# One written order from the first load to the end of stage two: a plan for stage one, sums of the scale in 64 columns, and differences of halves on GpSimd

## The chip, the cores and the metric

The kernel runs on one core of one Trainium2 chip. The metric is the time of one execution on the device in microseconds (us). A core has five engines that each work through a queue of their own in order: TensorE (PE in the profile, with its weight loads as PEld), VectorE (DVE), ScalarE (ACT), GpSimd (POOL) and SyncE (SP). SP, ACT and POOL also issue DMA transfers between DRAM and the on-chip memory (SBUF). Matrix products land in PSUM, 8 banks of 128 x 512 floats. An instruction waits by semaphore for what it reads, and for the buffer that it writes to come free; while it waits, everything behind it on its engine waits too.

## What is computed

```python
mod = (silu(c) @ w_mod).reshape(1, 6, 1, 512)          # c: (1, 512), w_mod: (512, 3072)
sa, ca, ga, sb, cb, gb = (mod[:, i] for i in range(6))
h = layernorm(x) * (1 + ca) + sa                       # x: (1, 2048, 512)
x = x + ga * irfft2(rfft2(h) * (w_r + 1j * w_i))       # a 2-D spectral filter
h = layernorm(x) * (1 + cb) + sb
x = x + gb * (mish(h @ w1 + b1) @ w2)                  # w1: (512, 1376), w2: (1376, 512)
```

## The kernel before

The 2048 rows are 128 partitions by 16 tiles n. The transforms are matrix products with constant matrices, in fp32 or as a high and a low fp32r part ("split"). There are three stages.

**Stage one** (the opening) goes over the 16 tiles. At the start the gate of `c` is made (`sc`), PE multiplies it with four pieces of `w_mod` (`scale_sums`, L333, 128 equal columns for each of four j into four banks), and DVE turns the constant `kr` into the scaled row transform `krs`, kr times one plus the sum (`scale_rows`, L338). `row_sums` multiplies ones by it, for the mean (`kb`). For each tile: loads of `x`, of the transposed `x` (`load_xt`) and of the column matrix `mraw` (`load_m`); PE's row transform (`p1_row`, L277, bank A or B); mean and variance on DVE and ACT (`norm_sums`, `first_guess`, `first_scale`); `p1_mean` on DVE; a high part (`p1_cast`, ACT) and a low part (`p1_low`, DVE, for the odd tiles in `POOL_LOW` on POOL inside `p1_cast`); the split of `mraw` into `mring` (`p1_split`: one cast on ACT, a difference and a negation on POOL); three groups of three matmuls in bank C (`p1_col`, L322 to L324); and a copy to `a_sb` (`p1_save`, L328, ACT). During the last tiles DVE sums the shift `sa` (`shift_sum`, L184), then PE transforms it (`shift_rows`, L348) and DVE keeps the part that each partition owns in `saz` (L355 and L357, first 16 columns, then 48).

**Stage two** (the middle) goes over 17 groups of columns of `a_sb`; group 0 is special, a full group has four columns and 512 elements. Group g passes through `turn_z` (four transposes on PE, L540), `copy_z` (ACT, L553), `p2_shift` (POOL adds `saz`, L558), `p2_mul` (PE with `kf`, L566), `lane` twice (ACT, L595 and L601), `other` (POOL times weights, L604), `own` (DVE times weights, L608), `p2_add` (DVE, L612), `fold` (step 0: difference of two halves, L622, on POOL for odd g below 15 and else on DVE; step 1 on DVE, L624), `spin_mul` and `spin_copy`, `p2_out` (PE, L480), and `store_d` twice (copies into `dd`, L458 on ACT, or L456 on DVE for the second copy of the groups in `FREE`). Between them the other vectors of `w_mod` are loaded (`mod_fetch`, SP) and summed (`mod_late`, L184, DVE), the filter's weights are reloaded (`load_wq`), and the gate `ga` goes through DRAM (`gate_flat`, `gate_spread`, L111) and is multiplied into `kiv` (`mod_gate`, L685, POOL).

**Stage three** transforms back (`p3_col`, L974; `p3_row`, L983, which reads `kiv`), normalizes again, and does the two dense layers with Strassen-like products (`up`, L1105; `down`, L1214) for the rest of the time.

What sets the order: inside `with tc.manual_schedule()` the instructions of an engine keep the order in which the program issues them. There are three such parts. Stage one's order is written out as a loop. The middle and the last stage are lists of steps (`Plan`), issued in the places that the long strings in `ORDERS` give. Between the three parts the framework's scheduler decides, so instructions of the next part can stand ahead of the end of the one before it.

Of the kernel before, what the change touches and what calls it, by code (L numbers as in the profile page):

```python
# [7 lines left out]
F32 = mybir.dt.float32  # L8
# [83 lines left out]
def tile_spectral_block(ctx: ExitStack, tc: tile.TileContext, x_d, w1_d, b1_d, w2_d,  # L92
# [156 lines left out]

    def load_all(n):  # L250
        load_xt(n)
        load_x(n)
        load_m(n)

    def load_rest():
        nc.sync.dma_start(kf, kf_d)
        nc.sync.dma_start(wz, wz_d)
        for i in range(4):
            nc.sync.dma_start(wqa[:, i], wq_d[i])
            if i == 1:  # L260
                nc.sync.dma_start(kv, kv_d)
# [33 lines left out]
    def p1_cast(n):  # L295
# [3 lines left out]
        if n in POOL_LOW:  # L299
            g = buf("t")  # L300
            if n == 1:
                nc.scalar.activation(gh, c, AF.Copy, scale=one)
# [1339 lines left out]
```

## Time and profile before

| | |
|---|---|
| median of three runs | 372.18 us (370.38 to 372.61) |
| profiled execution | 373.39 us, its span 371.6 |
| granted TensorE clock, mean | 0.994 |
| busy: PE, DVE, ACT, POOL | 355.2, 296.7, 248.3, 98.5 us |
| moved by DMA | 91.78 MB, mean 247 GB/s |
| loads of `x` and `xring` in stage one | 16 each, 256 KB, 4.8 us to landing |

A row of the profile names the line of the kernel (L322), the engine, the operation, what it writes and reads (buffer numbers left out) with shapes, and how often; then busy time and the mean in ns. A time in brackets is how long the engine had been idle before the instruction, and what ended that. "SPq" and "ACTq" are DMA issues on those queues. The granted clock is a share of full speed. Ends of matmuls are modelled, so a busy PE is not PE at its peak.

### The profile page before, as it was taken

How to read it: one execution, taken by the hardware profiler on the slowest of the kernel's cores; microseconds unless marked ns; L12 is line 12 of the kernel's file. 1: busy time of each engine (PE TensorE's matmuls, PEld its weight loads, DVE VectorE, ACT ScalarE, POOL GpSimd, SP SyncE). 2: the span in 40 equal slices, each digit the busy share in tenths (PEclk: the TensorE clock that was granted, in tenths of full speed). 3: DMA queues.
4: the chain of work that ended last, by engine and by line, in shares of the span. 5: the costliest groups of instructions: out<-in, count | busy, mean ns of one | idle time of the engine just before them, and what ended most of it. 6: DMA issues, size and time to landing. Idle time of an engine off the chain costs nothing.

```text
span 371.6 us, 7670 instructions
## 1 busy us (share of the span) xinstructions
PE 355.2 (96%) x2598; PEld 319.3 (86%) x2598; DVE 296.7 (80%) x708; ACT 248.3 (67%) x549; POOL 98.5 (27%) x156
## 2 busy tenths in 40 slices
PE   8999978898899999999999899999999999999995
PEld 8999955566699988788888789999999999999995
DVE  1898957998969889775777679998579895895896
ACT  1798848897378979884567696674676744545741
POOL 0578707776217360114202200004100000000000
PEclk9999989999999999999999999999999999999999
DMA  7999994565365997999999979767895986974023
GB/s 245 362 324 375 342 388 164 183 194 181 134 196 175 261 353 259 344 326 307 278 320 311 365 261 321 192 222 218 262 315 146 270 268 189 293 251 114 2 56 115
DMA packets 55639, 91.78 MB, mean 247 GB/s; under 512 B 7696, under 2 KB 21104, under 8 KB 55472
## 3 DMA queue, kind: packets, MB, share of 16 engines
q1 hardware_dynamic: 51168, 77.52, 62.6%
q0 software_dynamic: 2416, 7.87, 8.6%
q10 hardware_dynamic: 2016, 5.90, 5.2%
q8 instruction: 21, 0.34, 0.4%
q14 instruction: 18, 0.15, 0.1%
HBM read 70.03 MB, written 17.57 MB: 236 GB/s over the span
## 4 chain that ended last, share of the span: by engine, by line
PE 58%; DMA 14%; DVE 12%; ACT 4%; issue 4%; POOL 3%; SPq 3%; ACTq 0%; DVEq 0%; POOLq 0%
PE bank L1105 17%; PE bank L1214 17%; PE bank L1088 6%; PE bank L1206 4%; DMA modr<-in_B_w_dram 3%; DMA wm<-in_w_mod_dram 3%; PE bank L1151 3%; PE bank L1210 2%; DMA wqa<-in_w_q_dram 2%; PE bank L974 2%; PE bank L277 1%; PE bank L983 1%; DMA xring<-in_x_t_dram 1%; DMA x<-modr 1%; PE bank L333 1%
## 5 line engine op out<-in xcount | busy, mean ns | idle before, releaser
L1105 PE MATMUL bank<-hT,wr 128*128 128x256 f32 x360 | 51.5, 284 | 1.1 <-DMA wr<-w_S 1.1
L1105 PEld LDWEIGHTS bank<-hT,wr 128*128 128x128 f32 x360 | 47.0, 191 | 2.7 <-issue 0.9
L1105 PE MATMUL bank<-hB,wr 128*128 128x256 f32 x318 | 46.5, 285 | 1.9 <-ACT odd L1118 1.1
L1105 PEld LDWEIGHTS bank<-hB,wr 128*128 128x128 f32 x318 | 42.0, 191 | 4.3 <-ACT odd L1118 1.3
L1032 ACT CAST ah<-buf 128x512 fp32r<-128x512 f32 (+1 forms) x35 | 21.0, 607 | 13.5 <-PE bank L1214 6.7
L1273 POOL DMA_DIRECT2D x<-modr x5 | 4.4, 877 | 93.8 <-DVE buf L1175 27.8
L1033 DVE TENSOR_TENSOR al<-buf,ah 128x512 fp32r<-128x512 f32 (+1 forms) x35 | 23.4, 672 | 6.4 <-ACT ah L1032 6.3
L1214 PE MATMUL bank<-w2a,ah 128*128 128x256 f32 x119 | 25.9, 283 | 0.0
L1088 PE MATMUL bank<-hB,wr 128*128 128x512 f32 x96 | 24.2, 393 | 0.1
L1214 PE MATMUL bank<-w2b,ah 128*128 128x256 f32 x105 | 23.1, 283 | 0.0
L900 POOL DMA_DIRECT2D turned<-x x16 | 8.8, 564 | 48.0 <-DVE buf L1175 21.2
L1088 PEld LDWEIGHTS bank<-hB,wr 128*128 128x128 f32 x96 | 17.8, 188 | 4.1 <-ACT buf L976 0.6
L322 PE MATMUL bank<-buf,mring 128*128 128x512 f32 x48 | 20.7, 432 | 0.2 <-DVE buf L315 0.2
L1214 PEld LDWEIGHTS bank<-w2a,ah 128*128 128x128 f32 x119 | 19.8, 191 | 0.1
L1214 PEld LDWEIGHTS bank<-w2b,ah 128*128 128x128 f32 x105 | 17.9, 191 | 0.6
L480 PEld LDWEIGHTS bank<-kv,a_sb 128*64 128x64 f32 x252 | 13.6, 137 | 5.3 <-ACT d L458 2.4
L983 PE MATMUL bank<-kiv,buf 128*128 128x128 f32 x128 | 17.0, 278 | 0.6 <-DVE x L986 0.5
L974 PE MATMUL bank<-kc,d 128*128 128x128 f32 x128 | 16.7, 276 | 0.5 <-ACT d L458 0.5
L277 PE MATMUL bank<-modr,xring 128*128 128x128 f32 x128 | 16.7, 275 | 0.0
L1033 DVE TENSOR_TENSOR al<-even,ah 128x384 fp32r<-128x384 f32 (+1 forms) x15 | 8.7, 580 | 9.9 <-ACT ah L1032 9.9
L480 PE MATMUL bank<-kv,a_sb 128*64 128x128 f32 x252 | 15.7, 276 | 1.0 <-ACT a_sb L637 1.0
L1214 PE MATMUL bank<-w,ah 128*128 128x256 f32 x84 | 16.4, 284 | 0.0
(328 smaller groups left out, 1097.1 us busy)
## 6 DMA issues: line engine op xcount, KB each, us to landing
wr<-w_S SPq DMA_DIRECT2D x60, 256.0 KB, 4.1
wr<-w_A SPq DMA_DIRECT2D x45, 256.0 KB, 4.1
w_S<-hT SPq DMA_DIRECT2D x20, 256.0 KB, 4.1
x<-in_A_x_dram SPq DMA_DIRECT2D x16, 256.0 KB, 4.8
xring<-in_x_t_dram SPq DMA_DIRECT2D x16, 256.0 KB, 4.8
w_A<-wr SPq DMA_DIRECT2D x15, 256.0 KB, 4.4
x<-modr POOLq DMA_DIRECT2D x7, 512.0 KB, 5.9
out_dram<-x SPq DMA_DIRECT2D x7, 512.0 KB, 3.7
```

The costliest lines, as they stand in the source:

```text
L277: nc.tensor.matmul(pgv[:, j], data(j), krs[:, j, :].rearrange("p (c q) -> p c q", c=2), start=True, stop=True)
L322: nc.tensor.matmul(pa, m[:, a, 0:128], g, start=(i == 0), stop=False)
L480: nc.tensor.matmul(o[0:1] if a.shape[1] == 1 else o, a, b, start=(n == 0), stop=(n == len(products) - 1))
L974: nc.tensor.matmul(o, dj, kc[0][:, n, :], start=True, stop=True)
L983: nc.tensor.matmul(px[:, j * P:(j + 1) * P], e[:, j * P:(j + 1) * P], kiv[:, j, :], start=True, stop=True)
L1032: nc.scalar.copy(h, r)
L1033: nc.vector.tensor_tensor(l, r, plain(h), op=ALU.subtract)
L1088: nc.tensor.matmul(ups[i, t, f], ring[t, a][:, p, b, :], sides[int(a[2]) - 1][:, :, q, b, :], start=(a[2] == "1" and b == 0 and n == 0), s ...
L1105: nc.tensor.matmul(o, w[:, p, k, :], h[:, q, k, :], start=(first and n == 0), stop=(last and n == 5), skip_group_check=True)
L1151: nc.tensor.matmul(ups[i, 0][:FL], w1s[:, p, u, :], sides[u // 2][:, :, q, u % 2, :], start=(u == 0 and p + q == 0), stop=(u == 3 and p == ...
L1206: nc.tensor.matmul(out_ps[b][n], a[p][:, half + 2 * f], w, start=(t == 1 and f == 0 and i == 0), stop=(t == NT - 1 and f == 1 and i == 2), ...
L1214: nc.tensor.matmul(out_ps[b][n][:, 256 * half:256 * half + 256], a[p][:, e], w2[t][q][:, r], start=(t == 1 and half == 0 and i == 0), stop ...
```

## The change

Four things change.

1. **Stage one becomes a plan of 302 single steps**, issued in the places that a new first string in `ORDERS` gives; the strings of the other two stages are new as well. Large steps are cut so that each is work of one engine: `p1_split` into `p1_high`, `p1_rest` and `p1_minus`; `p1_low` also for the odd tiles; `p1_col` by its three parts; `row_sums` and its copy; the shift's end into `shift_pick`, `shift_rows` and two `shift_own`.
2. **The scale's sums** (`scale_sums`) use 64 equal columns instead of 128, and the four j share one bank. `scale_ones` adds one to the four sums; `scale_row` then multiplies `kr` by it, j = 0 and 2 on DVE, 1 and 3 on ACT.
3. **All stages are one ordered part**: one `manual_schedule` is entered ahead of stage one and stays. So all of stage one's steps stand ahead of all of stage two's on each engine, and those ahead of stage three's.
4. **Differences of halves**: `FOLD(g)` is true for all g below 14, so step 0 of groups 2, 4, ... 12 moves from DVE to POOL (groups 14 to 16 are on DVE). `FREE` becomes (2, 5, 7, 9): the second copy of group 2 moves to DVE, those of 11 and 13 to ACT.

Some places in the new order. On SP the identity and the first `mraw` stand ahead of `kr`. On DVE stage one ends with `shift_sum(2)`, `p1_low(15)`, `shift_sum(3)`, `shift_own` twice; stage two begins with `own(1)`, `p2_add(1)`, `own(2)`, `p2_add(2)`, `mod_late(0, 0)`, `own(3)`. On PE the first steps of stage two keep their order (groups 1, 2 and 3 are turned, then 1 and 2 multiplied). `lane(16, 0)` stands behind `own(14)`, ahead of the additions of groups 14 and 15. `gate_spread` stands on ACT's queue behind `store_d(12, 1)`.

```diff
 ORDERS = (
...
+    "0 2-3 32 4-5 11 9 1 6-7 34 33 8 35-38 10 12 49-50 39-40 13 42 299 41 14 19 17 43 45 51 44 15 55 46 18 47 23 60 "
...
-    def p1_split(n):
+    def p1_high(n):
+        nc.scalar.copy(mt(n)[:, 0, 0:256], mraw[:, n, :])
+
+    def p1_rest(n):
         m = mt(n)
-        nc.scalar.copy(m[:, 0, 0:256], mraw[:, n, :])
         nc.gpsimd.tensor_tensor(m[:, 1, 0:256], mraw[:, n, :], plain(m[:, 0, 0:256]), op=ALU.subtract)
+
+    def p1_minus(n):
+        m = mt(n)
         nc.gpsimd.tensor_scalar(m[:, :, 256:384], plain(m[:, :, 128:256]), -1.0, 0.0,
                                 op0=ALU.mult, op1=ALU.add)
...
-    def scale_sums(ks, ps):
-        for k in ks:
-            for j in range(4):
-                nc.tensor.matmul(ps[j][:, 0:P], wmc[:, k, j * P:(j + 1) * P], sc[:, k:k + 1].to_broadcast([P, P]),
-                                 start=(k == 0), stop=(k == 3))
-
-    def scale_rows(ps):
+    def scale_sums(k):
+        if k == 0:
+            st["one"] = bank("C")
+        ps = st["one"]
         for j in range(4):
-            nc.vector.scalar_tensor_tensor(krs[:, j, :], kr[:, j, :], ps[j][:, 0:1], kr[:, j, :],
-                                           op0=ALU.mult, op1=ALU.add)
+            nc.tensor.matmul(ps[:, 64 * j:64 * j + 64], wmc[:, k, j * P:(j + 1) * P], sc[:, k:k + 1].to_broadcast([P, 64]),
+                             start=(k == 0 and j == 0), stop=(k == 3), skip_group_check=True)
+
+    def scale_ones():
+        ps = st.pop("one")
+        st["one"] = one = small.tile([P, 4], F32, name="one")
+        nc.vector.tensor_scalar(one, ps[:, 0:256:64], 1.0, None, op0=ALU.add)
+
+    def scale_row(j):
+        one = st["one"][:, j:j + 1]
+        if j % 2:
+            nc.scalar.activation(krs[:, j, :], kr[:, j, :], AF.Copy, scale=one)
+        else:
+            nc.vector.tensor_scalar(krs[:, j, :], kr[:, j, :], one, None, op0=ALU.mult)
...
-    with tc.manual_schedule():
-        nc.sync.dma_start(sc, c_d.rearrange("b (p k) -> p (b k)", k=4))
...
+    put(p1_save, N2 - 1)
+    put(shift_rows)
+    put(shift_pick)
+    for lo, hi in ((0, 16), (16, NQ)):
+        put(shift_own, lo, hi)
+
+    ctx.enter_context(tc.manual_schedule())
+    opening.run(0)
...
-    FREE = (5, 7, 9, 11, 13)
+    FREE = (2, 5, 7, 9)
 
     def FOLD(g):
-        return g % 2 and g < 15
+        return g < 14
...
-    with tc.manual_schedule():
-        nc.scalar.copy(scp, scb)
-        middle.run(0)
+    nc.scalar.copy(scp, scb)
+    middle.run(1)
...
-    ctx.enter_context(tc.manual_schedule())
...
-    plan.run(1)
+    plan.run(2)
```

More of the change, by code (lines that the diff above doesn't have):

```diff
@@ L298, in p1_cast @@
         gh, gl = buf("g1", F32R), buf("g2", F32R)
+        st["g", n] = gh, gl
+        if n not in POOL_LOW or n == 1:
+            nc.scalar.activation(gh, c, AF.Copy, scale=one)
         if n in POOL_LOW:
-            g = buf("t")
-            if n == 1:
-                nc.scalar.activation(gh, c, AF.Copy, scale=one)
+            st["gt", n] = g = buf("t")
             nc.scalar.activation(g, c, AF.Copy, scale=one)
@@ L344, in shift_rows @@
     def shift_rows():
-        ps = bank("D")
+        st["shift"] = ps = bank("D")
         pgv = ps.rearrange("p (c d q) -> p d c q", c=2, d=4)
@@ L446, in tile_spectral_block, with spread_copy @@
-        p1_save(N2 - 1)
-        shift_rows()
+    def spread_copy():
+        nc.scalar.copy(scb, st.pop("scb"))
+    put(load, sc, c_d.rearrange("b (p k) -> p (b k)", k=4))
+    put(table)
+    for k in range(4):
+        put(load, wmc[:, k, :], wm_d[1, k])
+    put(load, kr, kr_d)
+    put(load_xt, 0)
+    put(load_x, 0)
+    put(load_m, 0)
+    put(load_xt, 1)
+    put(load, ident, kp_d)
+    for n in range(1, 8):
+        put(load_x, n)
+        put(load_m, n)
+        if n < 7:
+            put(load_xt, n + 1)
@@ new lines, in tile_spectral_block, with split_steps, load_steps, rest_steps @@
+    put(set_ones)
+    put(gate)
+    put(warm, 6)
+    for k in range(4):
+        put(scale_sums, k)
+    put(scale_ones)
+    for j in range(4):
+        put(scale_row, j)
+    def split_steps(n):
+        put(p1_high, n)
+        put(p1_rest, n)
+        put(p1_minus, n)
+    def load_steps(n):
+        put(load_xt, n)
+        put(load_x, n)
+        put(load_m, n)
+    def rest_steps():
+        put(load, kf, kf_d)
+        put(load, wz, wz_d)
+        for i in range(4):
+            put(load, wqa[:, i], wq_d[i])
+            if i == 1:
+                put(load, kv, kv_d)
+                put(load, kw, kw_d)
+                put(load, kiv, ki_d)
+                put(load, b1n[:, 0:NF - 1], b1_d[0:(NF - 1) * P].rearrange("(f p) -> p f", p=P))
+                put(load, b1n[0:F - (NF - 1) * P, NF - 1:NF], b1_d[(NF - 1) * P:F].unsqueeze(1))
@@ new lines, in tile_spectral_block @@
+    put(norm_sums, 2)
+    for n in range(N2):
+        if n >= 1 and n != 2:
+            put(p1_save, n - 1)
+        if n + 2 < N2:
+            put(p1_row, n + 2)
+            if n == 2:
+                put(p1_col, 1, 2)
+                put(p1_save, 1)
+            if n + 10 < N2:
+                load_steps(n + 10)
+            if n == 4:
+                put(load, wms, wm_d[0].rearrange("k p e -> p k e"))
+            if n == 6:
+                rest_steps()
+        if 1 <= n and n + 1 < N2:
+            put(p1_mean, n + 1)
+            if n % 2:
+                put(first_scale, n + 1, n + 3)
+            put(p1_cast, n + 1)
+            if n + 1 in POOL_LOW:
+                put(p1_low, n + 1)
+        for i in range(n + 2 + (n > 5), min(n + 3 + (n > 4), N2)) if n else ():
+            split_steps(i)
+        if n and n not in POOL_LOW:
+            put(p1_low, n)
+        for i in range(2) if n == 1 else range(3):
+            put(p1_col, n, i)
+        if n + 3 < N2:
+            put(norm_sums, n + 3)
+            if n % 2 == 0:
+                put(first_guess, n + 2, n + 4)
+        if 11 <= n < 15:
+            put(shift_sum, n - 11)
```

187 lines of the change are left out of this document (68 added, 119 removed), and 114 rows, old and new, of the table ORDERS.

## The prediction

> **What bounds the kernel now.** I read the busy times of stretches first, one stretch for each stage; columns are the stretch in us, its length, the busy time (and instructions) of PE, weight loads, DVE, ACT and POOL, the granted clock, the DMA share and GB/s.
>
> ```profile
> span 371.6 us, 7670 instructions
> 8.63:49.95 41.32, 41.12 (x300) 38.16 (x299) 36.41 (x96) 33.12 (x76) 27.88 (x39) 1.00 1.03 353
> 55.59:102.38 46.79, 41.86 (x376) 28.23 (x375) 41.03 (x83) 34.38 (x85) 29.36 (x43) 0.99 0.53 171
> 102.38:371.60 269.22, 261.54 (x1870) 243.66 (x1870) 214.91 (x515) 177.67 (x384) 40.56 (x67) 1.00 0.76 241
> 200.00:220.00 20.00, 17.64 (x113) 15.15 (x112) 14.27 (x36) 15.78 (x29) 2.19 (x4) 1.00 0.96 339
> 360.00:371.60 11.60, 7.64 (x51) 6.83 (x49) 8.16 (x17) 1.55 (x3) 0.00 (x0) 0.97 0.43 126
> ```
>
> Stage one (8.63 to 49.95) has PE busy for 41.12 of 41.32 us, and stage three for 261.54 of 269.22. In stage three 3.96 of the 7.68 idle us lie in the last 11.60, where the output goes out, and 2.36 between 200 and 220. Reordering can win little in either. Stage two has PE idle for 4.93 of 46.79 us and DVE for 5.76. What stands out is the seam, 49.95 to 55.59, which I read in the order of time; columns are start, length, engine, line, operation, and in brackets the idle time before it with what ended it.
>
> ```profile
> 48.90 1.05 PE L348 MATMUL bank<-kr,cols 128*128 128x128 f32 x8
> 49.79 1.72 PE L540 MATMUL bank<-ident,a_sb 128*128 128x128 f32 x11
> 50.33 1.02 ACT L553 COPY early<-bank 128x384 f32<-128x384 f32 x2 [0.64 <-PE bank L540]
> 51.60 0.69 DVE L184 SCALAR_TENSOR_TENSOR wm<-wm,bank 128x512 f32<-128x512 f32 x1 [3.15 <-DMA wm<-in_w_mod_dram]
> 52.82 0.29 DVE L355 TENSOR_TENSOR modr<-bank,pick 128x128 f32<-128x128 f32 x1
> 53.14 0.37 DVE L357 TENSOR_REDUCE saz<-modr 128x16 f32<-128x128 f32 x1
> 53.66 0.51 POOL L558 TENSOR_TENSOR early<-early,saz 128x3 f32<-128x3 f32 x3 [7.05 <-DVE saz L357]
> 53.91 3.22 PE L566 MATMUL bank<-early,kf 128*128 128x384 f32 x4 [2.40 <-POOL early L558]
> 55.59 0.49 ACT L595 ACTIVATE wide<-bank 64x384 f32<-64x384 f32 x1 [3.46 <-PE bank L566]
> 73.22 1.02 PE L566 MATMUL bank<-wide,kf 128*128 128x512 f32 x2
> 52.00:54.00 2.00, 0.09 (x1) 0.09 (x1) 1.94 (x7) 0.14 (x1) 0.34 (x3) 0.86 1.04 399
> 54.00:56.00 2.00, 2.00 (x3) 1.08 (x4) 0.80 (x1) 0.41 (x1) 0.17 (x2) 0.50 1.01 398
> ```
>
> The shift's products (L348) end at 49.95 and their sums (L355, L357) need only them, yet start at 52.82: two `mod_late` steps of stage two stand ahead of them on DVE, and the first waits 3.15 us for its weights from DRAM. Everything follows: POOL adds the shift at 53.66, PE multiplies from 53.91 after an idle 2.40 us, and its four matmuls take 3.22 us, where two usually take 1.02, because the granted clock is 0.50 between 54 and 56. No engine is busy here; the wait bounds.
>
> **The seam (gain 3.3 us).** In the new order both `shift_own` steps belong to the first list and all of it stands ahead of the second, where the first `mod_late` comes behind `p2_add(2)`. So the first shift sum runs at 49.95 + 0.1, takes 0.29 + 0.37 and is done at 50.7. The copy of group 1 (half of the 1.02 from 50.33) ends at 50.8, and the shift is added by about 51.1. PE turns groups 1 to 3 until 49.79 + 1.72 = 51.51, then multiplies group 1. That is late next: PE's own transposes. Two matmuls at 1.02 end at 52.53, and ACT's first `lane` starts near 52.5, against 55.59 (3.1 earlier); the second group's product ends at 51.51 + 2.04 = 53.55, against 53.91 + 3.22 = 57.13 (3.6 earlier). I take 3.3. The other shift sum lies beside PE's products; the copy of the scale's row (`scp`), now behind ACT's last save instead of ahead of it, lies beside the first transposes. Bounds: 2.4 if only the idle time of PE goes and the clock still drops; 4.0 if everything behind follows the second group with no slack lost. A `mod_late` that still waits would now hold only `own(3)` and what is behind it on DVE; its weights had landed by 51.60 and group 3 comes after that.
>
> **Start of stage one (loss 0.2).**
>
> ```profile
> kr<-in_kr_dram SPq DMA_DIRECT2D x1, 256.0 KB, 5.0
> 3.05 0.43 SPq L370 DMA_DIRECT2D kr<-in_kr_dram  x1
> 4.00 4.80 PE L333 MATMUL bank<-sc,wmc 128*128 128x128 f32 x32
> 8.16 1.16 DVE L338 SCALAR_TENSOR_TENSOR modr<-kr,bank 128x128 f32<-128x128 f32 x4 [4.97 <-PE bank L333]
> ```
>
> The sums shrink from 128 to 64 columns. At the present 4.80 / 32 = 0.15 us for each matmul, halving would save 2.4 us, but the four weight pieces are loaded one after the other, so I count only the last quarter (8 of 32, 1.2 us), which can end up to 0.6 earlier. Against that `kr` now queues behind the identity (128 x 128 floats, 64 KB) and the first `mraw` (128 x 256, 128 KB). It landed at 3.05 + 5.0 = 8.05; with 0.19 MB more at 353 GB/s it lands at 8.6, with two more issues of 0.43 at 8.9. The new `scale_ones` lies beside that wait (uncovered it is at most one of today's scalings, 1.16 / 4 = 0.29). The four row scalings are shared by DVE and ACT. The first row product then starts near 8.85 instead of 8.63. Ends: 0.3 earlier if `kr` is not late, 0.9 later if both issues and bytes count in full.
>
> **Body of stage one (gain 0.3).** Nothing is taken from PE. Its 41.32 us hold 16 tiles of 2.3, which makes 36.8 us,
>
> ```profile
> 20.33 0.89 PE bank L277 x8
> 21.22 0.23 PE bank L322
> 21.45 0.12 PE bank L323
> 21.57 0.12 PE bank L324
> ```
>
> (rows from the chain of waits: 0.89, and three times 0.23 + 0.12 + 0.12 = 1.41 a tile), plus three more products of 0.89 (the row sums, the scale's spread, the shift): 39.5. At most 1.8 us of small stretches can go. I take 0.3; ends 0 and 1.0 gained. The steps of ACT, DVE and POOL and the loads change places beside PE. SP's queue is full (share 1.03), but PE waits for nothing but 0.2 us today, so a load that moves by a place or two costs nothing; one that came 1 us after its product would cost that 1 us, and the start's upper end covers it.
>
> **Body of stage two (gain 1.5).** Six differences of halves, those of the even groups 2 to 12, leave DVE for POOL; five copies on DVE become four.
>
> ```profile
> L622 DVE TENSOR_TENSOR a_sb<-a_sb 128x252 f32<-128x252 f32 x9 | 5.6, 627 | 0.0
> L622 POOL TENSOR_TENSOR a_sb<-a_sb 128x252 f32<-128x252 f32 x6 | 4.6, 769 | 0.0
> L456 DVE COPY d<-bank 128x256 f32<-128x256 f32 x5 | 2.1, 418 | 1.0 <-ACT d L458 1.0
> 96.19 0.69 DVE L593 SCALAR_TENSOR_TENSOR wide<-bank,wqb 64x512 f32<-64x512 f32 x1
> 102.38 2.05 PE L974 MATMUL bank<-kc,d 128*128 128x128 f32 x16 [0.47 <-ACT d L458]
> ```
>
> DVE loses 6 x 0.627 + 0.418 = 4.2 us and falls from 41.0 to 36.9; POOL gains 6 x 0.769 = 4.6 and rises from 29.4 to 34.0; ACT gains one copy. PE's 41.86 us are now the floor, so of DVE's 4.2 us at most the 4.93 that PE stands idle can matter. Where DVE ends PE's waits is the tail: from 96.19 on DVE does the last group alone, and PE waits for it. `lane(16, 0)` moves ahead of three additions and five folds. I take 1.5 of the 4.93. Ends: 3.5 gained (nearly all the idle time), 1.5 lost (DVE waits for POOL's differences in its queue).
>
> **The gate behind the stage (loss 0.3).**
>
> ```profile
> modr<-ga ACTq DMA_DIRECT2D x1, 256.0 KB, 6.1
> 90.80 0.34 ACTq L111 DMA_DIRECT2D modr<-ga  x1
> 95.86 0.92 ACT L458 COPY d<-bank 128x256 f32<-128x256 f32 x3 [2.17 <-DVE d L456]
> 96.97 1.55 POOL L685 TENSOR_TENSOR kiv<-kiv,modr 128x512 f32<-128x512 f32 x1 [2.97 <-DMA modr<-ga]
> 104.30 1.13 PE L983 MATMUL bank<-kiv,buf 128*128 128x128 f32 x8
> modr<-gb ACTq DMA_DIRECT2D x1, 256.0 KB, 4.3
> ```
>
> `gate_spread` moves on ACT's queue from 90.80 to behind the store of group 12, about 96.5 by the row at 95.86. Today its product ends at 98.52 and `p3_row(0)` uses it at 104.30: 5.78 us of cover, of which the move takes 5.7. A shorter tail then shows through, unless the transfer lands in 4.3 like its sister instead of 6.1. I take 0.3; ends 0 and 1.5.
>
> **Stage three (0).** Its 1154 steps are the same, and PE's work with them; they stand ten places from where they were on average. The loads of its first `w2` now wait on SP's queue behind `second_in`, whose buffer comes free with the last group; behind them wait the loads of `w1`, which need that space too. `split_w2(1)`, which uses the first, moves from behind the third of PE's column and row steps to behind the twelfth, and that covers it. Ends: 2.0 gained (nearly the 2.36 between 200 and 220), 1.5 lost (as much again as the small waits).
>
> **Sum.** 0.2 - 0.3 - 3.3 - 1.5 + 0.3 + 0 = -4.6 us. The profiled execution took 373.39 us (span 371.6 and 1.8 around it), 1.21 over the median of the three runs, 372.18. So 368.8 by the profiled one, and **367.6** by the median, 1.2% faster. One per cent is 3.7 us, about what can be told from no change here; the runs differ by 2.2.
>
> **A rule against the change.** What the trace shows first:
>
> ```profile
> 80.39 1.27 POOL L604 TENSOR_TENSOR buf<-buf,wqa 128x512 f32<-128x512 f32 x1 [0.73 <-POOL wide L558]
> 80.90 1.03 DVE L622 TENSOR_TENSOR a_sb<-a_sb 128x252 f32<-128x252 f32 x1
> 99.07 0.42 DVE L622 TENSOR_TENSOR a_sb<-a_sb 128x252 f32<-128x252 f32 x1
> ```
>
> The same DVE step takes 0.42 us alone and 1.03 while POOL multiplies. The Trainium skill, "SBUF — State Buffer", section "SBUF: two separate sides", says that a DVE operation with two SBUF inputs and a GpSimd operation exclude each other for a whole instruction; the two rows agree. As an estimate by that rule, each of the six moved folds would still hold DVE for its whole time, DVE would lose nothing, the body's 1.5 would go, and the sum would be -3.1, or 369.1; the sum above does not use this.
>
> **The rivals.**
> - *Forecast* (0.50): 367.6, own range 366.0 to 369.0.
> - *More goes* (0.15): PE's idle time in stage two goes nearly whole and the waits at 200 to 220 with it, 2.0 + 2.0 more: 363.6. For it: no engine but PE is near its floor. Against: each group still passes through four engines in turn.
> - *Given back* (0.22): the seam gains 3.3, but the tail gains nothing, the gate is 1.5 late and the start 0.9: 3.3 + 0.3 - 1.5 - 0.9 = 1.2, so 371.0.
> - *Transfers keep the seam* (0.07): the DMA share is 1.04 and 1.01 between 52 and 56, so group 1 may wait for `kf` or `wqa` instead. Then the edit does not do what it says; without the 3.3 the sum is 1.3, so 370.9. Against: these loads stand ahead of stage two's, whose first landed by 51.60.
> - *DVE stands behind POOL* (0.06): a group's second fold, in DVE's queue, waits for its first on POOL, and that for a product of 1.27 us ahead of it, 1.27 + 0.77 = 2.0 in all; every addition queued behind it waits too. DVE has 5.76 + 4.2 = 10 us to spare over 13 folds, 0.77 each. Beyond that each us counts against the 3.1 us that are left of the sum without the body's 1.5: the point is 13.1 / 13 = 1.0 us for each fold. At 1.5 us it is 13 x 1.5 - 10 - 3.1 = 6.4 slower, 378.6. For it: the row at 80.90. Against: the new order puts most first folds several steps ahead of the second.
>
> The range 364.5 to 372.0 leaves out the last rival, somewhat over half of the second, and the worst fifth of the two cases near 371. Faster by over 1% (below 368.5): four fifths of the forecast and all of the second, 0.55. Slower by over 1%: 0.06. The rest, 0.39.
>
> **What would show it.** Right: no `mod_late` ahead of the shift's sums on DVE, the first `kf` product within 2 us of the shift's, a granted clock of 1.0 there; stage two 45 us long with DVE near 37 and POOL near 34; `p3_row(0)` waiting for POOL under 0.5 us. Wrong: PE waiting for a DMA at the seam, DVE rows released by POOL's folds for over 5 us, the row products starting after 9.5, or PE idle over 9 us in stage three.

## The result and the profile after

The changed kernel takes **375.09 us** in the median of 20 executions (370.98 to 377.5), the kernel before 372.44 us in the median of 20 beside them: ratio 1.0072, 95% interval 1.0045 to 1.0098. It is 0.7% slower, where 367.6 us and 1.2% faster had been forecast. The profiled execution took 373.97 us, span 372.2. The intervals leave out executions over 1.5% above the fastest of the same kernel, and since kernels with 64-column sums turn out to have two kinds of starts, that can leave out part of one kind (of after2, below, the longest four), so for them the medians of all executions are the safer numbers. The two profiled executions lie only 0.6 us apart: the one of before stood 0.95 us above its median, that of the changed kernel 1.12 below.

First the stretches of the changed kernel: stage one from its first row product, the seam with the first group of stage two, the rest of stage two, stage three. Columns are as in the prediction.

```profile
12.15:53.99 41.84, 41.84 (x298) 39.51 (x299) 36.03 (x94) 32.22 (x77) 25.53 (x37) 1.00 1.02 357
53.99:57.60 3.61, 3.48 (x21) 2.45 (x20) 2.32 (x5) 3.16 (x7) 1.04 (x5) 1.00 0.98 381
57.60:102.76 45.16, 40.52 (x369) 27.23 (x368) 38.14 (x81) 34.09 (x84) 33.48 (x48) 1.00 0.52 168
102.76:372.20 269.44, 261.22 (x1870) 243.60 (x1870) 215.65 (x515) 178.02 (x384) 40.75 (x67) 1.00 0.78 241
```

Stage three begins at 102.76, before at 102.38: whatever the seam won is gone again by then. The loss stands at the very beginning, where stage one starts at 12.15 in place of 8.63; from there to the end of the row products it grows to 5.2 us (16.84 against 11.65). The timeline of TensorE in the changed kernel:

```profile
3.94 3.65 PE L336 MATMUL bank<-sc,wmc 128*128 128x64 f32 x16
7.91 3.67 PE L336 MATMUL bank<-sc,wmc 128*128 128x64 f32 x16 [0.32 <-DMA wmc<-in_w_mod_dram]
12.15 2.08 PE L276 MATMUL bank<-modr,ones 128*128 128x128 f32 x8 [0.57 <-DVE modr L349]
14.03 2.82 PE L276 MATMUL bank<-modr,xring 128*128 128x128 f32 x16
```

The sums (L336; 16 products, each recorded as two matmuls) were meant to take half as long as the old ones, and the 32 matmuls take 7.32 us in place of 4.80. That is 0.23 us each. And the row products behind them (L276), whose work nobody touched, are slow too: 24 take 4.69 us (12.15 to 16.84), against 2.86 before (8.80 to 11.65; the first overlaps the sums). That one matmul and its neighbours are slow alike points to the pace of TensorE itself. Counting instructions in stretches of 2 us shows it (the column behind the brackets is the granted clock):

```profile
5.00:7.00 2.00, 2.00 (x12) 1.00 0.87 274
13.00:15.00 2.00, 2.00 (x11) 1.00 0.90 307
16.00:18.00 2.00, 2.00 (x20) 1.00 1.07 399
```

11 or 12 matmuls in 2 us until 15 us, of 64 columns as of 128, and 20 from 16 us on, while the granted clock is recorded as 1.00 all through. The busy share is no help either: TensorE counts as fully busy in all three. Only the count, or the spacing of equal matmuls, shows the two paces. By the starts of the single matmuls in the trace they stand 213 ns apart until 15.7 us, the sums as well as the row products, and 112 ns apart from then on.

The seam did what was forecast:

```profile
52.93 1.05 PE L363 MATMUL bank<-kr,cols 128*128 128x128 f32 x8
54.02 0.29 DVE L369 TENSOR_TENSOR modr<-bank,pick 128x128 f32<-128x128 f32 x1 [1.54 <-PE bank L363]
55.38 1.67 PE L647 MATMUL bank<-early,kf 128*128 128x384 f32 x4
56.23 0.49 ACT L676 ACTIVATE wide<-bank 64x384 f32<-64x384 f32 x1
```

The shift's sums (L369) follow its products at once, no weighted sum of `mod_late` stands ahead of them, and the first `lane` (L676) comes 2.25 us after the products' end, before 5.64.

### The profile page after: what moved, and what is told of

The parts are those of the page before. It is cut to its first block, busy times and chain, and to the rows that moved or that the text cites. A ratio compares the mean times of both kernels' runs of the same rounds, so it can differ in the third digit from the quotient of the medians.

```text
span 372.2 us, 7651 instructions
## 1 busy us (share of the span) xinstructions
PE 357.3 (96%) x2598; PEld 322.4 (87%) x2598; DVE 293.3 (79%) x700; ACT 249.7 (67%) x552; POOL 102.1 (27%) x162
## 4 chain that ended last, share of the span: by engine, by line
PE 77%; DMA 8%; DVE 6%; ACT 4%; issue 2%; SPq 1%; ACTq 0%; DVEq 0%; POOL 0%; POOLq 0%
PE bank L1172 18%; PE bank L1281 18%; PE bank L1155 6%; PE bank L276 5%; PE bank L561 3%; DMA wr<-w_S 3%; PE bank L324 3%; PE bank L647 3%; PE bank L1041 3%; PE bank L1218 3%; PE bank L1050 3%; PE bank L1273 2%; PE bank L1277 2%; DMA x<-modr 2%; DMA wmc<-in_w_mod_dram 2%
## 5 line engine op out<-in xcount | busy, mean ns | idle before, releaser
L276 PE MATMUL bank<-modr,xring 128*128 128x128 f32 x128 | 17.6, 284 | 0.0
L1050 PEld LDWEIGHTS bank<-kiv,buf 128*128 128x128 f32 x128 | 15.6, 191 | 1.2 <-ACT buf L1043 1.1
L266 POOL TENSOR_TENSOR mring<-mraw,mring 128x256 fp32r<-128x256 f32 x16 | 11.7, 738 | 17.6 <-ACT mring L262 17.6
L276 PEld LDWEIGHTS bank<-modr,xring 128*128 128x128 f32 x128 | 16.5, 202 | 0.0
```

Source lines behind the costliest of these rows:

```text
L266: nc.gpsimd.tensor_tensor(m[:, 1, 0:256], mraw[:, n, :], plain(m[:, 0, 0:256]), op=ALU.subtract)
L276: nc.tensor.matmul(pgv[:, j], data(j), krs[:, j, :].rearrange("p (c q) -> p c q", c=2), start=True, stop=True)
L1050: nc.tensor.matmul(px[:, j * P:(j + 1) * P], e[:, j * P:(j + 1) * P], kiv[:, j, :], start=True, stop=True)
```

## The experiments

The table has every kernel's milestones from its one profile, in us; "seam" is the end of the shift's products to the first `lane`, "stage two" from there to the first `p3_col`. Medians are of 12 executions (20 in the first two rows), beside the kernel before on the same chip; the kernels of one set ran on one chip, so kernels are compared within a set.

| kernel | set | median (before) | ratio, 95% interval | first row product | seam | stage two | `p3_col` | span |
|---|---|---|---|---|---|---|---|---|
| before | 0 | 372.44 | | 8.63 | 5.64 | 46.79 | 102.38 | 371.6 |
| after | 0 | 375.09 (372.44) | 1.0072, 1.0045 to 1.0098 | 12.15 | 2.25 | 46.53 | 102.76 | 372.2 |
| a128 | 1 | 370.20 (371.38) | 0.9961, 0.9939 to 0.9984 | 9.47 | 2.25 | 46.50 | 98.31 | 368.2 |
| b64 | 1 | 371.73 (371.38) | 1.0000, 0.9975 to 1.0024 | 8.67 | 4.64 | 46.05 | 100.71 | 369.8 |
| awarm | 1 | 371.18 (371.38) | 0.9977, 0.9949 to 1.0005 | 9.98 | 2.24 | 46.50 | 98.80 | 369.4 |
| bone | 1 | 371.98 (371.38) | 1.0012, 0.9984 to 1.0040 | 8.30 | 2.25 | 47.39 | 99.19 | 368.8 |
| after2 | 2 | 373.70 (372.04) | 0.9975, 0.9929 to 1.0020 | 12.12 | 2.25 | 46.50 | 103.05 | 375.6 |
| a64four | 2 | 373.96 (372.04) | 1.0027, 0.9987 to 1.0067 | 9.01 | 2.25 | 46.51 | 97.88 | 367.1 |
| b64one | 2 | 374.57 (372.04) | 1.0064, 1.0032 to 1.0096 | 11.90 | 2.26 | 46.04 | 102.90 | 372.3 |
| a128_fold | 2 | 372.77 (372.04) | 1.0010, 0.9976 to 1.0044 | 9.41 | 2.25 | 50.88 | 103.40 | 372.9 |
| a128_again | 3 | 370.53 (371.75) | 0.9978, 0.9950 to 1.0006 | 9.76 | 2.24 | 46.51 | 98.60 | 368.1 |
| a128_fold2 | 3 | 372.40 (371.75) | 1.0018, 0.9986 to 1.0050 | 9.55 | 2.25 | 48.09 | 100.01 | 370.8 |
| b64_again | 3 | 372.50 (371.75) | 1.0006, 0.9978 to 1.0034 | 10.98 | 2.25 | 46.06 | 101.34 | 370.6 |
| best | 3 | 370.63 (371.75) | 0.9961, 0.9931 to 0.9990 | 9.67 | 2.24 | 46.52 | 98.98 | 370.0 |
| bone2 | 4 | 371.46 (372.91) | 0.9974, 0.9947 to 1.0002 | 8.21 | 2.25 | 48.57 | 100.25 | 369.7 |
| bone_fold | 4 | 371.55 (372.91) | 0.9999, 0.9969 to 1.0030 | 8.94 | 2.25 | 49.68 | 102.11 | 370.8 |
| b_fold | 4 | 373.89 (372.91) | 1.0037, 1.0004 to 1.0070 | 9.13 | 4.01 | 48.00 | 102.36 | 374.1 |
| best2 | 4 | 370.30 (372.91) | 0.9947, 0.9917 to 0.9976 | 8.11 | 2.24 | 46.51 | 97.82 | 366.0 |

In the profiles of a128_fold (granted clock 0.94 from 50 to 100 us), bone2 (0.96 in stage two) and bone_fold (0.97) the clock fell for a while inside stage two; the other stage-two lengths stand at 1.00, that of before at 0.99.

### The columns of the scale's sums

**a128**: the changed kernel with 128 columns.

```
-            nc.tensor.matmul(ps[:, 64 * j:64 * j + 64], wmc[...], sc[:, k:k + 1].to_broadcast([P, 64]),
+            nc.tensor.matmul(ps[:, P * j:P * j + P], wmc[...], sc[:, k:k + 1].to_broadcast([P, P]),
...
-        nc.vector.tensor_scalar(one, ps[:, 0:256:64], 1.0, None, op0=ALU.add)
+        nc.vector.tensor_scalar(one, ps[:, 0:512:128], 1.0, None, op0=ALU.add)
```

> The changed kernel with scale's sums in 128 columns again (the four j side by side in one bank), nothing else changed. Theory, slow array: the 64-column matmuls don't keep TensorE busy enough for its matmuls to go over to the fast pace, which before came at about 5.2 us and after at about 16 us; with 128 columns the sums take about 4.8 us again, the first row product starts near 8.9 us (12.15 after, 8.63 before), the first 24 row products take 2.9 us (4.7 after), and the time is about 5 us below the changed kernel's (ratio to before about 0.987). Rival, loads and order: the first row product is late because the new order asks for the four kr tiles and mraw in other places, or because one bank is shared by the four j; then the sums still end near 11.6 us and the time stays within 0.5 us of the changed kernel (ratio about 1.007).

The timeline of a128:

```profile
3.80 5.09 PE L336 MATMUL bank<-sc,wmc 128*128 128x128 f32 x32
9.47 1.16 PE L276 MATMUL bank<-modr,ones 128*128 128x128 f32 x8 [0.57 <-DVE modr L349]
10.46 1.95 PE L276 MATMUL bank<-modr,xring 128*128 128x128 f32 x16
```

The counts of TensorE in stretches of 2 us of a128:

```profile
4.00:6.00 2.00, 2.00 (x10) 1.00 0.83 250
6.00:8.00 2.00, 2.00 (x18) 1.00 0.99 360
```

TensorE goes over to the fast pace at about 6.5 us, in the middle of the sums, some 9 us earlier than in the changed kernel. Twice the columns, and the sums take 5.09 us in place of 7.32; the untouched row products behind them are fast again. Stage three begins 4.45 us earlier than in the changed kernel (98.31 against 102.76). The ratio 0.9961 against 1.0072 is 1.1%, some 4 us of the 5 expected. The first row product came 0.6 later than expected; see best2.

**b64**: the kernel before with 64 columns in its four banks (`ps[j][:, 0:64]`, `to_broadcast([P, 64])`), and **b64_again**, the same kernel on another chip.

> The kernel before with one edit: scale's sums in 64 columns, their four banks kept, old order and all else as before. Theory, slow array: the sums take 7 us or more in place of 4.8, the first row product starts 3 us or more later than 8.63, the first row products run at the slow pace (440 ns in the mean where 297 stood), and the kernel is about 5 us slower than before (ratio about 1.013). Rival, loads and order or the shared bank: none of these is in this kernel, so the first row product starts at 8.6 us or earlier and the ratio is 1.000 or a little below.

> The kernel before with 64-column sums in four banks once more, on another chip. Theory, filling by columns alone: which executions start slowly depends on where the stretches that are judged begin, so here some executions out of twelve take 3 to 5 us more, as 11 of 12 did with one bank; the ratio rises to 1.003 or above. Theory, banks: four banks keep the fast start in the order of before; then no more than one execution of twelve is slow and the ratio is within 0.3% of 1.

The timeline of b64:

```profile
4.12 4.56 PE L333 MATMUL bank<-sc,wmc 128*128 128x64 f32 x32
8.67 1.29 PE L277 MATMUL bank<-modr,ones 128*128 128x128 f32 x8
```

The same of b64_again:

```profile
4.13 7.06 PE L333 MATMUL bank<-sc,wmc 128*128 128x64 f32 x32 [0.16 <-DMA wmc<-in_w_mod_dram]
10.98 2.02 PE L277 MATMUL bank<-modr,ones 128*128 128x128 f32 x8
```

The theory failed on b64: no loss, ratio 1.0000. The very same kernel has a late start in its second profile. So the 64 columns alone don't decide; with them the start was early in one profile and late in the other. And a late start costs the kernel before little: b64_again's shift products end 3.0 us later than b64's (53.03 against 50.02), its first `lane` 0.6 later (55.28 against 54.66). The seam, which waits until about 51.5 us for the weights of `mod_late`, takes up the rest, 4.64 us becoming 2.25. The changed kernel has no such wait, and a late start goes through to the end.

**awarm**: the changed kernel with `put(warm, 12)` in place of `put(warm, 6)` (24 recorded matmuls of 128 columns ahead of the sums in place of 12), 64 columns kept.

> The changed kernel with 12 warming matmuls of 128 columns ahead of the sums in place of 6, sums in 64 columns kept. Theory, slow array: the six more matmuls (about 1.5 us at the slow pace of 0.25 us each) bring the fast pace before the sums begin or soon after; the 64-column sums then take at most 4 us, the first row product starts at 9 to 10.5 us, the first 24 row products take 2.9 us, and the time is 3 to 5 us below the changed kernel's (ratio to before about 0.995). Rival, 64 columns are slow in themselves (the weight load of each sets the pace): the sums take 7 us or more as now and end no earlier, and the time is the changed kernel's or up to 1.5 us above it.

The timeline of awarm:

```profile
5.72 3.68 PE L336 MATMUL bank<-sc,wmc 128*128 128x64 f32 x32
9.98 1.16 PE L276 MATMUL bank<-modr,ones 128*128 128x128 f32 x8 [0.58 <-DVE modr L349]
```

With these ahead, TensorE goes over to the fast pace at 5.2 us, still among the warming matmuls, the same 64-column sums take 3.68 us, 0.115 each, and all 12 spans lie within 368.1 to 370.9. So 64 columns aren't slow in themselves, and the rival falls.

**after2** (the changed kernel unedited), **a64four** (its sums in the four banks `[bank(tag) for tag in "CCBB"]` in place of one `bank("C")`) and **b64one** (the kernel before with the changed kernel's one bank).

> The changed kernel once more, unedited, for a second profile and more times beside the kernels of this call. Theory, window: TensorE goes over to the fast pace only when a stretch of some 3 us has been filled well enough (1.6 to about 5 us in four of the profiles so far); the 64-column sums at the slow pace fill it too little, so in most executions the fast pace comes at about 16 us and in a few at 5 to 9 us. The median then stands about 4 us above the kernel with 128 columns (ratio to before about 1.007), with single runs near it. Rival, accident: the profile of the changed kernel was one unlucky execution and the times a property of the other chip; then the ratio falls to 0.997 to 1.000 here.

> The changed kernel with its 64-column sums in four banks, as before had them, in place of one shared bank (scale_ones then reads four columns from four banks, four small instructions in place of one, at most 0.3 us more). Theory, shared bank: the sums of the kernel before in 64 columns and four banks went over to the fast pace at 5 us, so it is the shared bank that keeps the array slow; the first row product then starts near 9 us and the time is 4 us below the changed kernel's (ratio to before about 0.996). Theory, filling: the number of columns alone counts, and the kernel before got through by its phase or its wait for wmc; then the fast pace still comes at about 16 us in most executions and the ratio stays at about 1.007.

> The kernel before with the changed kernel's sums: 64 columns, the four j in one bank; order and loads as before. Theory, shared bank: the sums take 7 us, the first row product starts near 12 us and the ratio to before is about 1.010. Theory, filling by columns alone or the new order: like the kernel before with 64 columns in four banks, ratio within 0.3% of 1, first row product near 8.7 us.

After2's 12 spans fall in two groups, five from 366.7 to 369.2 and seven from 371.8 to 375.6; its median of 373.70 stands 1.66 above before. In the first 20 executions of the changed kernel three spans were below 371 and 17 at 372.0 or more. A64four has four from 367.1 to 369.9 and eight from 372.0 to 374.1; its profile caught an early one (first row product 9.01, span 367.1). One bank or four makes no difference that can be told in the changed kernel. B64one started late in its profile (11.90) and has one span below 371.0 among twelve; its seam, with nothing changed in it, is 2.26 us. The spans of after2 and a64four say: at 64 columns the start is early or late by the execution, mostly late, and in the changed kernel the shared bank doesn't set it. How often b64 starts late can't be read from its spans, since its seam takes up most of a late start. Whether four banks help under the old order stays open: b64one is slower than b64 by intervals that don't overlap (on another chip), and b64_again's late start shows at least that four banks don't prevent it. A pause of TensorE for the weights `wmc` doesn't decide either: the changed kernel waits 0.32 us for them, a64four 0.36 us and starts early all the same.

No profile of a kernel with 128 columns starts late, under either order, and the 24 spans of a128 and a128_again form one group (366.6 to 370.9). The starts of the single matmuls show when TensorE goes over to the fast pace: between 4.9 and 7.1 us in all eleven profiles with 128-column sums, at 4.3 and 5.3 in a64four and b64, and only between 13.8 and 17.0 in b64_again, after, b64one and after2, when 2.8 to 4.9 us of 128-column row products had run.

### Where the rest of the seam's gain went

**bone** and **bone2**: the kernel before with only the single ordered part.

```
-    with tc.manual_schedule():
-        nc.scalar.copy(scp, scb)
-        middle.run(0)
+    nc.scalar.copy(scp, scb)
+    middle.run(0)
...
-    ctx.enter_context(tc.manual_schedule())
```

(the same line stands at the opening part instead)

> The kernel before with one edit: the single ordered part over all stages, with the old orders, the old sums and the difference where it was. Theory, the seam: the stretch from the end of shift_rows to the first lane, 5.64 us before and 2.25 after, shrinks to 2.3 to 3 us, and the kernel is about 3 us faster than before (ratio about 0.992). Rival, the seam was closed by the new order of stage one and not by the single part: the stretch stays above 5 us and the ratio is within 0.2% of 1.

> The kernel before with the single ordered part over all stages, once more, as the base for the two kernels beside it. Theory, given back on DVE: the seam is about 2.3 us (5.64 before, 4.64 in another profile), stage two about 47.4 us in place of 46.05, stage three unchanged, so that 0.5 to 1.5 us are left (ratio to before 0.996 to 1.001). Rival, accident of the other chip with its low clock (0.995 in the median): the whole seam's gain is seen, ratio 0.993 or below.

The seam closes to 2.25 us both times, the first `lane` comes at 51.80 and 51.68 in place of 54.4 to 55.6, and yet the ratios are 1.0012 and 0.9974. Stage two of b64, whose second stage is that of before:

```profile
54.66:100.71 46.05, 41.12 (x375) 28.02 (x373) 41.02 (x83) 34.40 (x85) 29.29 (x43) 1.00 0.54 178
```

Stage two of bone:

```profile
51.80:99.19 47.39, 41.22 (x375) 28.03 (x374) 43.38 (x87) 34.39 (x85) 29.66 (x44) 1.00 0.56 192
```

TensorE does the same work; VectorE has 2.36 us more, and the stretch is 1.34 longer. Two groups of VectorE grew by over 1 us each. One is the weighted sums of `mod_late`, in b64:

```profile
L184 DVE SCALAR_TENSOR_TENSOR wm<-wm,bank 128x512 f32<-128x512 f32 x5 | 3.3, 678 | 0.0
```

And in bone:

```profile
L184 DVE SCALAR_TENSOR_TENSOR wm<-wm,bank 128x512 f32<-128x512 f32 x7 | 4.6, 678 | 0.0
```

Two weighted sums that used to be done in the seam, where everybody waited, now run in the stretch. They don't lengthen it: they lie at its very beginning (51.54 to 52.83), and the copy behind them starts 1.29 us after the first `lane` in both kernels. The other group is the second folds (L624 in b64, L625 in bone). Counted from the first `lane`, the first twelve of sixteen start within 0.02 us of each other in the two kernels, and the thirteenth too (38.42 and 38.41 us). That one takes 0.41 us in b64 and 1.76 in bone; all that follows on VectorE is 1.35 later, and the stage is 1.34 longer. Rows of b64 (those of folds hold two each, the thirteenth and the next):

```profile
93.08 0.75 DVE L624 SCALAR_TENSOR_TENSOR a_sb<-a_sb 128x252 f32<-128x252 f32 x2
94.95 1.55 POOL L685 TENSOR_TENSOR kiv<-kiv,modr 128x512 f32<-128x512 f32 x1 [2.60 <-DMA modr<-ga]
```

And of bone, where TensorE waits for what comes of the fold:

```profile
89.98 1.72 POOL L686 TENSOR_TENSOR kiv<-kiv,modr 128x512 f32<-128x512 f32 x1 [0.52 <-DMA modr<-ga]
90.21 2.09 DVE L625 SCALAR_TENSOR_TENSOR a_sb<-a_sb 128x252 f32<-128x252 f32 x2
93.10 0.39 PE L634 MATMUL bank<-a_sb,kv 128*128 128x8 f32 x2 [1.25 <-ACT d L459]
```

In bone GpSimd's product with the gate (`mod_gate`) begins 0.23 us before the fold, and the fold ends 0.27 us after the product; in b64 the product comes behind these folds and meets none. The transfer of the gate is issued at the same place of the stage in both, 34.5 us after the first `lane`, but lands after 3.65 us in bone and 5.75 in b64. Bone2 and bone_fold have the same fold at 1.76 us beside the same product. So in the traces the seam's closing lost 1.34 us in one meeting of VectorE and GpSimd; no run moves the gate's product alone. Stage three of bone still begins 1.52 us before that of b64.

**bone_fold** and **b_fold**: bone and before with the difference of the halves on GpSimd for every group below 14.

```
     def FOLD(g):
-        return g % 2 and g < 15
+        return g < 14
```

> The kernel before with two edits: the single ordered part, and the difference of the halves on GpSimd for every group below 14. Theory, given back on DVE: with the differences gone from DVE (six of 0.63 us) there is room for the two weighted sums that moved into stage two, so stage two takes 46.0 to 46.5 us and the kernel is 1 to 1.5 us faster than its neighbour without the second edit (ratio to before 0.992 to 0.996). Rival, TensorE's waits at the end of stage two (2.1 us for ScalarE's d) have another cause: stage two stays at 47.4 us and the two are equal.

> The kernel before with the difference of the halves on GpSimd for every group below 14, and nothing else. Theory, DVE isn't the bound of stage two while the two weighted sums run in the seam: stage two stays at 46.0 us within 0.4 and the ratio is within 0.2% of 1. Rival, DVE's relief shortens the stage by itself, as my prediction had it: 1 to 1.5 us less, ratio about 0.996.

Both theories fall. Under the old order the moved differences cost time: b_fold's stage two is 48.00 us against 46.05, ratio 1.0037 (1.0004 to 1.0070), and bone_fold gains nothing on bone2. The waits of b_fold's stage two (us in total, times, longest):

```profile
DVE a_sb L624 <- POOL a_sb L622: 3.0, 4, 1.3
```

VectorE stands 3.0 us in front of second folds whose first folds GpSimd hasn't done: the mechanism of the prediction's last rival, small. Of the 1.95 us, 0.77 have come when the fifteenth second fold starts; that fold meets the gate's product and takes 1.60 us, which is the rest. So the theory of bone_fold looked for a load on VectorE where one meeting made the loss, and moving the differences didn't remove it.

**a128_fold** and **a128_fold2**: the reverse, a128 (new order) with the differences of the even groups back on VectorE.

> The changed kernel with 128-column sums, and the difference of the halves back on VectorE for the even groups (fold on GpSimd only for odd groups below 15, as before). Theory, stage two is bound by TensorE and its waits for ScalarE: the stretch from the first lane to the first p3_col, 46.50 us with the difference on GpSimd, stays within 0.7 us and the ratio to before is 0.996 to 0.998. Rival, VectorE's relief is what made the stretch as short as it is: it grows by 1.5 us or more and the ratio rises to 1.000 or above. Third, GpSimd's slower instructions cost as much as VectorE saves: the stretch shrinks by 0.5 us or more and the ratio falls to 0.994 or below.

> 128-column sums, and the difference of the halves back on VectorE for the even groups, beside the same kernel with it on GpSimd. Theory, VectorE's relief is worth something in this order: stage two, 46.50 us with the difference on GpSimd, takes about 47.5 us and the kernel is 1 to 2 us slower than its neighbour (ratio to before near 1.000). Rival, no effect: within 0.5 us of the neighbour, and the difference between the two runs so far lay in the granted clock (0.991 in the profiled one).

Stage two of a128_again:

```profile
52.09:98.60 46.51, 41.89 (x375) 28.08 (x373) 38.36 (x80) 35.36 (x86) 34.11 (x50) 1.00 0.57 199
```

Stage two of a128_fold2, on the same chip:

```profile
51.92:100.01 48.09, 42.35 (x375) 28.04 (x373) 41.93 (x87) 35.37 (x86) 29.91 (x44) 1.00 0.56 189
```

1.58 us longer, and 1.87 in the medians (372.40 against 370.53). In the new order stage two is shorter with the differences on GpSimd, in the old one with them on VectorE: each loses 1.6 to 2.0 us with the other's placement (1.2 of the 1.95 in the meeting with the gate's product). Exchanged together, as the change does it, they give 46.5 against 46.05: nothing won, 0.45 lost.

### A better version

**best**: a128 with the old start: four banks, no `scale_ones`, each row scaled on VectorE straight from its bank. **best2**: best with `kr` loaded ahead of the identity and the first `mraw`.

```
-    "0 2-3 32 4-5 11 9 1 6-7 34 33 8 35-38 ...
+    "0 2-3 32 4-6 11 9 1 7 34 33 8 35-38 ...
```

> The changed kernel with the old start of the scale: 128-column sums in four banks, no scale_ones, each row scaled on VectorE straight from its bank as in the kernel before. Theory, the step between the sums and the first row product (0.57 us idle on TensorE with scale_ones) goes: first row product near 8.8 us instead of 9.47, and the time 0.5 us below its neighbour with scale_ones (ratio to before about 0.995). Rival, kr or the weight pieces land late and set the start: first row product stays at 9.2 us or later and the time is the neighbour's.

> The kernel named best (128-column sums in four banks, rows scaled from their banks), with the load of kr put back ahead of the identity and the first mraw on SyncE's queue. Theory, kr: it landed at 9.1 us in best and the first scaling waited for it; issued 0.95 us earlier it lands near 8.1, the first row product starts at 8.6 to 8.9 instead of 9.67, and the time is 0.5 to 0.9 us below best (ratio to before 0.993 to 0.995). Rival, the transfers share one bandwidth, so that what is put ahead delays what stands behind it by as much: the first row product comes earlier but the first mraw or x is late, and the time is that of best (0.996).

VectorE's first scalings in best, from its timeline:

```profile
9.26 0.62 DVE L343 SCALAR_TENSOR_TENSOR modr<-kr,bank 128x128 f32<-128x128 f32 x2 [6.06 <-DMA kr<-in_kr_dram]
```

The same in best2:

```profile
7.64 0.80 DVE L343 SCALAR_TENSOR_TENSOR modr<-kr,bank 128x128 f32<-128x128 f32 x2 [4.44 <-PE bank L336]
```

Best missed its theory because `kr` set the start, as its rival had it; with `kr` earlier VectorE waits for the sums again and the first row product comes at 8.11. Best2 is faster than the kernel before: 370.30 us, ratio 0.9947 (0.9917 to 0.9976). Against best the half per cent expected can't be told, nor a gain on a128 (370.20 and 370.53): the intervals overlap, and they ran on different chips.

## Why the prediction was wrong

- **Start of stage one** (loss 0.2, measured 3.52 and 1.7 more in the row products behind it): this is the step that failed. The prediction took the sums' time from the columns, at 0.15 us a matmul, counted what halving them could save, and let only `kr` speak against it; its upper end was 0.9. The 0.15 was a mean over two paces, the slow one until 5.9 us and the fast one behind it. The profiles show that halving saves next to nothing at either pace: 0.22 us a sum at the slow pace (7.06 / 32 in b64_again) where 128 columns take 0.24 (2.93 / 12 warming matmuls in a128), 0.115 (3.68 / 32 in awarm) against 0.119 (3.81 / 32 in bone) at the fast one; start to start the matmuls of both widths stand 213 ns apart at the one pace and 112 at the other. Rows of the timelines, a128 first:

```profile
1.04 2.93 PE L377 MATMUL bank<-ones 128*128 128x128 f32 x12 [1.04 <-DVE b1n L406]
```

And bone:

```profile
4.65 3.81 PE L333 MATMUL bank<-sc,wmc 128*128 128x128 f32 x32 [0.68 <-DMA wmc<-in_w_mod_dram]
```

And it usually puts off the change from one pace to the other: with 128 columns TensorE went over during the sums (a128), in the changed kernel at about 16 us, after some 3.7 us of 128-column row products. The prediction's own sign of being wrong, row products starting after 9.5, came up. That TensorE must be filled by enough columns for a while before it goes over fits a128, awarm and the late starts; what exactly counts no run here shows, and why two executions of one kernel differ stays open.

The Trainium skill, "TensorE: Matmul & The Clock Gate", section "Part 1: The HAM clock gate (the "warmup" mystery)", says that TensorE's clock starts at half rate and goes to full rate after a busy window of about 3.4 us that runs freely, so that the point varies from run to run. The traces agree in kind: in a128 TensorE is slow from 1.04 to about 6.5 us and then goes at nearly twice the pace, and the point differs between executions of equal kernels (b64 and b64_again). They don't agree for the 64-column sums: by that rule a TensorE busy from 1.04 us on is fast by 7.9 at the latest (an estimate: two windows of the 3.4 us that the Trainium skill gives), and the changed kernel's, recorded as busy but for pauses of 0.32 and 0.57 us, was slow until 15.7. The same page of the Trainium skill puts the cost of the ramp below 1% of a typical kernel; here a late start cost about 4 us of 372.

- `kr` behind the identity and `mraw`: right in kind. With fast sums the start was 9.47 and 9.76 (0.8 and 1.1 late), about the step's upper end, of which the loads' order is the part that best2 removed.
- **Body of stage one** (gain 0.3): under-sized. a128's first row product to the end of the shift's products is 40.10 us against 41.32, so 1.2 gained; in the changed kernel the slow row products hid it (41.84). The share of 1.03 that the prediction reads as SyncE's queue is that of the DMA engines.
- **The seam** (gain 3.3, measured 3.39): right, by the steps given. Half a correction: before's profiled execution had its clock at half there; at full clock b64 has 4.64 and b_fold 4.01, so the usual gain is 1.8 to 2.4, at or below the step's lower end.
- **Body of stage two** (gain 1.5, measured 0.26 against the profiled execution and a loss of 0.45 against b64 at full clock): wrong in mechanism too. The relief came: VectorE, which the prediction had falling from 41.0 to 36.9, fell to 38.5 with two weighted sums more. That is against the prediction's estimate in *A rule against the change*, by which VectorE would lose nothing, though single folds do stand still beside a product of GpSimd (1.76 us in bone). But TensorE's idle time in the stage hardly followed, from 4.93 to 4.64 us, so VectorE's load wasn't what most of it waited for. The tail didn't get shorter: 5.65 us from VectorE's last `lane` (L680) to stage three, before 5.49 (L599). What bounds the stage stays open.
- **The gate** (loss 0.3): 0. The transfer was issued late, but landed 3.2 us after its issue in place of 6.1, and its product ends at 102.22 with 2.5 us of cover left:

```profile
97.41 0.33 ACTq L122 DMA_DIRECT2D modr<-ga  x1
100.66 1.56 POOL L766 TENSOR_TENSOR kiv<-kiv,modr 128x512 f32<-128x512 f32 x1 [5.76 <-DMA modr<-ga]
104.68 0.57 PE L1050 MATMUL bank<-kiv,buf 128*128 128x128 f32 x3
```

- **Stage three** (0): 269.44 against 269.22. Right.
- The rivals: *Given back* (371.0) came nearest in kind, the seam's gain being spent again, but in the start and not in the tail and the gate. Its start of 0.9 is what a128 shows, and a128's 370.2 and 370.5 are close to its time. *DVE stands behind POOL* is real under the old order only. None held a slow start, and the range ended 3 us below the result.
- With fast sums the rest of the forecast still doesn't come out: against b64, a128 starts 0.80 later, has a body of stage one 1.25 shorter, a seam 2.40 shorter and a stage two 0.45 longer, so that stage three begins 2.4 us earlier, and its median is 1.2 below before's where 4.6 had been forecast.

## What to carry to other kernels

Before making the first matmuls of a kernel smaller, look at how long equal matmuls take there and when they become faster; work that only fills TensorE at the start may be what makes everything behind it fast, and a wait further down can hide its loss in one kernel and not in the next. When a gain is lost again further down, lay the two traces beside each other, counted from one common step, before blaming a load that grew: in bone twelve folds agreed to 0.02 us and the thirteenth held the whole loss. An order written out by hand and the placement of its steps on engines belong together: measured singly, either half of this pair lost 1.6 to 2.0 us of its stage.

## What the hardware showed unexpectedly

The pace of equal matmuls differed by nearly two (213 ns against 112 from start to start at 128 columns) while the granted clock was recorded as 1.00: at the start of a kernel the spacing tells the pace and that column doesn't. A matmul of 64 columns with a new 128 x 128 weight tile stood as far from the next as one of 128 columns, at both paces. One kernel, unedited, had its first row product at 8.67 us in one execution and at 10.98 in another (b64 and b64_again, on two chips); the spans of the changed kernel fall into two groups some 5 us apart (366.7 to 369.2 and 371.8 to 375.6 in after2), which fits such starts, though both its profiles caught a late one. And a fold of 0.41 us on VectorE took 1.76 when a product of 1.72 us on GpSimd had begun 0.23 us before it.
